# A two-layer decode kernel whose planner gets a new model of transfers, instruction fetches and matmul activity

## The chip, the core and the metric

The kernel runs on one core of a Trainium2 chip. The metric is device time in microseconds (us), lower is better. Every time below is of a whole execution on the device, or comes from one execution taken by the hardware profiler.

## What is computed

Two kinds of layer alternate, A, B, A, B, each added to its input, for 8 sequences of one token (width 448). Both A layers use the same weights and the same caches; so do both B layers.

```python
def _A_ref(x, k_cache, v_cache, wq, wo):      # B=8, 16 query heads, 8 cached heads, 4096 keys, 256 wide
    q = (x @ wq).reshape(B, Sq, Hq, Dh).transpose(0, 2, 1, 3)
    k = jnp.repeat(k_cache, 2, axis=1); v = jnp.repeat(v_cache, 2, axis=1)
    p = _softmax(jnp.einsum("bhqd,bhkd->bhqk", q, k) * Dh ** -0.5)
    o = jnp.einsum("bhqk,bhkd->bhqd", p, v)
    return o.transpose(0, 2, 1, 3).reshape(B, Sq, Hq * Dh) @ wo
def _B_ref(x, w1, w2, w3, w4):
    # the token-mixing part shifts along a sequence of length 1 and so adds nothing
    x1 = x + hs
    return x1 + _gelu(_layernorm(x1) @ w3) @ w4
x = x + _A_ref(_layernorm(x), ...)
x = x + _B_ref(_layernorm(x), ...)
x = x + _A_ref(_layernorm(x), ...)
x = x + _B_ref(_layernorm(x), ...)
```

The caches are large: 8 rows of 8 heads, with 2 MiB of keys and 2 MiB of values for each head, in bfloat16. One row's keys and values are 32 MiB, and both A layers need them.

## The kernel before

**Data.** On chip there is room for 30 quarter slots (`QUARTERS`) of 512 KiB in the tile `kv`; a head's keys or values are four such quarters. A load (`issue_kv`, line 625) fetches one to four quarters of a head that lie side by side, in one transfer of 128 rows. Of each row's eight heads, heads 3 to 7 are "kept": their keys stay on chip from layer 1 to layer 2 (`KEEP_K` 5, but for two quarters that are held otherwise), and so do six quarters of values (`KEEP_V`). Heads 0 to 2 are "free": everything of theirs is loaded for each layer anew.

**Work of one head.** `front` takes keys: TensorE transposes each quarter in two pieces (line 1250) into the tiles `psT`, VectorE or ScalarE copies them back (lines 1233 and 1234), scores follow (line 1045, "scr", 8 matmuls to a group), then maximum, exponentials and sums. `back` takes values: four groups of 8 matmuls (line 1132, "pv"), one for each quarter, then the parts are added (1146, 1148, 1156) and a part of the output projection is made (1181, "wor"). A score group of layer 2, or of a key that isn't kept, frees its quarter slot, and so does each value group of a quarter that isn't kept. The next load into that slot waits for it.

**Between the layers of one row.** After the eighth head of layer 1 the last part of the output projection (`wo_mm`, "wo", lines 985 and 988) closes the row's attention; `mid` then makes sums (731), the MLP's first product (`h_mms`, 56 matmuls at line 839), its second (985, 988), and the queries of layer 2 (823). Only then can layer 2's scores of this row begin. While this goes on, the values of the next row's free heads in layer 1 are loaded and multiplied (`run([("b", 0, b + 1, h) for h in free_heads])`), and then layer 2 of this row starts with its kept heads.

**The planner.** The order of everything is not written out by hand. `Plan.op` records each operation with an estimated time and what it reads and writes; `Plan.schedule` then simulates the engines and puts the operations of each engine into an order. The order is fixed at build time; `synchronise` adds the semaphore waits. A load's size is decided there too: `next_kv` asks for as many quarters as are left of the head and as its `most` allows; it takes them if so many free slots lie side by side before the time `late`, when the transfers issued so far are about to run out, and else takes fewer:

```python
late = max(free["sp"], dma_end - self.LEAD)
...
t = max(late, times[0])
m = min(m, max(k for k, a in runs(t)))
```

The transfers are one queue in this model, with one time `dma_end`. SP (SyncE) issues all loads, in the planned order, so a load that waits holds up those behind it. Fetches of instructions (`fetched`) delay TensorE alone.

**The clock of TensorE.** The planner counts the matmul columns of each window of 3.413 us; above `COLS` it takes the short durations, else the long ones. Where TensorE would stand idle and the count is under `TARGET` it puts in "fillers" (line 1457, "warm"): matmuls whose result nobody reads.

`MOST` is the largest number of quarters in one load of a free head's values in layer 1, for every row but the first.

Of the kernel before, what the change touches and what calls it, by code (L numbers as in the profile page):

```python
# [31 lines left out]
BOOST = None  # L32
HOTK = 7
L2 = (3, 4, 2, 1, 0)
MOST = 4
MOST2 = 4
BACKS = (0, 3, 6)
MIX = "KKKKKFFF"
# [1 line left out]
PV0 = 0  # L40
PV1 = DH
QW, HW, YW = 24, 24, 12
SC = 448
YC = 0
SB, SR = 64, 128
# [30 lines left out]
class Plan:  # L76
# [5 lines left out]
    HOT = 3500  # L82


    ISSUE, LEAD = 4.0, 5.0
    BLOCK, FETCH = 128, 6.0
    LAT = {"pe": 0.25, "dve": 0.06, "act": 0.06, "pool": 0.05, "sp": 0.4}

    def __init__(self):
        self.ops = []  # L90
# [41 lines left out]
    def fetched(self, t, d, n, pairs, next_block):  # L132

        per = d / n
        while n:
            room = self.BLOCK - pairs % self.BLOCK
            if room == self.BLOCK:
                t = max(t, next_block)
                next_block = t + self.FETCH
            k = min(n, room)  # L140
            pairs += k
            n -= k
            t += k * per
        return t, pairs, next_block

    def schedule(self):
        engs = ["pe", "dve", "act", "pool", "sp"]
        free = {e: 0.0 for e in engs}
# [16 lines left out]
        for o in self.ops:  # L165
            if not left[o]:
                release(o, 0.0)
        dma_end = 0.0
        win, cols, warm = 0, 0, False
        recent, hot = [], False  # L170
        bank_ev = {}
# [5 lines left out]
        n = 0  # L177
# [14 lines left out]
        def next_kv(i):  # L192

            u = sp_next[i].unit
            m = 1
            while m < u.most and i + m < len(sp_next) and sp_next[i + m].unit is not None and \
                    sp_next[i + m].unit.tile is u.tile and sp_next[i + m].unit.u == u.u + m and \
                    sp_next[i + m].unit.keep == u.keep:  # L200
                m += 1
            late = max(free["sp"], dma_end - self.LEAD)
            times = sorted(set(x for x in self.free_at if x < 1e9))
            if not times:
                return None
            for t in [max(free["sp"], times[0])] + [x for x in times if free["sp"] < x <= late]:
                fit = [(k, a) for k, a in runs(t) if k >= m]
                if fit:
                    break
            else:  # L210
                t = max(late, times[0])
                m = min(m, max(k for k, a in runs(t)))
                fit = [(k, a) for k, a in runs(t) if k >= m]

            before = sp_next[i - 1].unit if i else None
            if before is not None and before.tile is u.tile:
                for k, a in fit:
                    if a <= before.slot + 1 <= a + k - m:
                        return t, m, before.slot + 1
            k = min(k for k, a in fit)  # L220
            fit = [a for k2, a in fit if k2 == k]
            q = min(fit) if u.keep else max(fit) + k - m
            return t, m, q

        while n < len(self.ops):
            best = None
            for e in engs:
                if e == "sp":
# [5 lines left out]
                    if sp_i < len(sp_next) and sp_next[sp_i] in ready:  # L234
                        t = max(free[e], ready[sp_next[sp_i]])
# [7 lines left out]
                if avail[e]:  # L243
                    t = free[e]
                elif pend[e]:
                    t = max(free[e], pend[e][0][0])
# [4 lines left out]
            t, e = best  # L251
            if e == "sp":
                o = sp_next[sp_i]
# [74 lines left out]
            order[e].append(o)  # L328
            n += 1
            if e == "sp":  # L330
                free[e] = t + 0.45
                start = max(t + self.ISSUE, dma_end)
                dma_end = start + o.dur
                end = dma_end
            else:
                d = o.dur
                if e == "pe":

                    w = int(t / self.WIN)
                    while win < w:  # L340
                        warm = cols >= self.COLS
                        cols = 0
                        win += 1
                    cols += d[2]
                    recent.append((t, d[2]))
                    end, pairs, next_block = self.fetched(t, d[0] if warm else d[1], d[3],
                                                          pairs, next_block)
                    d = end - t
                elif isinstance(d, dict):
                    d = d[e]  # L350
                end = free[e] = t + d
# [109 lines left out]
def bass_interleave_layers__gqa_block_cached__mixer_s_mlp__decode_kernel(  # L461
# [20 lines left out]
    plan = Plan()  # L482
# [117 lines left out]
        return bass.AP(tensor=ap.tensor, offset=ap.offset, ap=[list(x) for x in ap.ap[:-1]] + [[0, P]])  # L600


    FASTER = 1.05

    def dma(name, dst, src, nbytes, sem, val, wr, at, row=8192):

        us = nbytes / 16 / 26.88e3 + nbytes / row / 16 * 0.008
        plan.op("sp", lambda eng: eng.dma_start(dst, src), us / FASTER, name, wr=wr, prio=at,
                dma=(sem, val))

    def dma_once(name, parts, keys, at, also=()):
# [7 lines left out]
    def issue_kv(o, n, q):  # L619

        (cache, b, h), u = o.unit.tile, o.unit.u
        src = cache[b, h].rearrange("(m s) d -> m (s d)", m=P)[:, u * 2048:(u + n) * 2048]
        dst = kv[:, q * 2048:(q + n) * 2048]
        slot_n[q] += 1
        o.emit = lambda eng: eng.dma_start(dst, src)  # L625
        o.dma = (slot_sem[q], 16 * slot_n[q])
        o.dur = ((n << 15) / 26.88e3 + 8 * 0.008) / FASTER

    plan.issue_kv = issue_kv

# [63 lines left out]
    def pe(fn, n, rd=(), wr=(), banks=(), name="chain", prio=None, width=20):  # L694

        if prio is None:
            prio = urge[0] + len(plan.ops)
        d = 0.06 + 0.026 * n
        return plan.op("pe", fn, (d, max(d, 0.06 + n * width / 1200), width * n, n), name, rd=rd, wr=wr, banks=banks, prio=prio)

    def mark(o):

# [298 lines left out]
    def front(layer, b, h, prio=None):  # L1001
# [29 lines left out]
        for u in range(4):  # L1031
            if u in fresh:
                for pc in range(2):
                    bank = transpose_piece(ks[u], pc, u in hold)
                    if u in hold:
                        held.setdefault(u, []).append(bank)

            typ, half = u % 2, u // 2

            def sc(t, typ=typ, q=ks[u]):  # L1040
                last = None
                for c in range(2):
                    w = qb[:, h, c, 2 - 2 * typ:6 - 2 * typ]
                    for g in range(4):
                        last = t.matmul(ps[32 * g:32 * g + 4, SR:SR + DH], w,  # L1045
                                        slot_ap(q, g * 512, 512)[:, c:512:2],
                                        start=(typ == 0 and c == 0), stop=(typ == 1 and c == 1),
                                        skip_group_check=True, tile_position=(0, 32 * g))
                return last
            o = plan.op("pe", sc, (0.25, 0.46, 512, 8), "scr",  # L1050
                    rd=qk + ["q0", ("s", ks[u], 0), ("s", ks[u], 1)],
                    wr=[("sr", half)] + [("sc", par, x) for x in range(u, 4)], banks=[bk],
                    prio=prio and prio + len(plan.ops))
            if layer and h == first2[b] and u == 3:
                o.hot = False
            if u in back_in:
                for pc, bank in enumerate(banks_of[back_in[u]]):
                    evacuate(ks[u], pc, bank).tbank = bank
                    held_banks.remove(bank)
            elif u not in keep_k:  # L1060
                o.frees = ks[u]
            hi = len(plan.ops) - 10 ** 5
            if typ:
                def out_rows(e, half=half):
                    if e is nc.vector:
                        return e.tensor_copy(sR[half][:, :], ps[:, SR:SR + DH])  # L1066
                    return e.copy(sR[half][:, :], ps[:, SR:SR + DH])  # L1067
                plan.op("ev", out_rows, {"dve": 0.42, "act": 0.4}, "evh", rd=[("sr", half)], wr=[("sR", half)],
                        banks=[bk], prio=hi)

                def turn_s(t, half=half):
                    last = None
# [35 lines left out]
    def back(layer, b, h):  # L1108
# [15 lines left out]
        for u in range(4):  # L1124

            def pv(t, u=u, q=vs[u]):
                last = None
                for s in range(8):
# [4 lines left out]
                                    slot_ap(q, s * 256, 256), start=(i < 4), stop=(i >= 28),  # L1133
                                    skip_group_check=True, tile_position=(0, g4))
                return last
            o = plan.op("pe", pv, (0.25, 0.46, 512, 8), "pv",
                    rd=[("pT", nr, 0), ("pT", nr, 1), ("s", vs[u], 0), ("s", vs[u], 1),
                        "pz"],
                    wr=[("pv", par, x) for x in range(u, 4)], banks=[bk])
# [35 lines left out]
        if k < HKV:  # L1175
            def wo_row(t):
                last = None
                for i in range(4):
# [4 lines left out]
                                    stop=(k == HKV - 1 and i >= 2),  # L1183
                                    skip_group_check=True, tile_position=(0, r))
                return last
            o = plan.op("pe", wo_row, (0.41, 0.78, 448, 4), "wor", rd=[("oT", no), "wo0"], wr=[kr],
                        banks=["R"], prio=hi)
            if k == HOTK and layer == 0:
                o.hot = True
# [327 lines left out]
```

## Time and profile before

| | |
|---|---|
| three executions | 1109.34, 1109.49, 1111.36 us (median 1109.49) |
| the profiled execution | 1109.86 us; span of its instructions 1108.1 us |
| TensorE (PE) | busy 970.0 us (88%), granted clock 0.94 of full speed |
| VectorE (DVE), ScalarE (ACT), GpSimd (POOL) | 618.0, 337.3 and 100.1 us |
| read from memory | 438.38 MB, 396 GB/s over the span |
| transfers of instructions | 127 packets, 2.08 MB, 0.8% of the 16 engines' span |
| chain that ended last | PE 51%, DMA 40%, DVE 6% |
| loads of 2048, 1536, 1024 and 512 KiB | 135, 7, 82 and 91 |

The chain that ended last is followed back from the last instruction, at each step to what released it. Busy shares are averages over stages: what bounds a stage is read in windows of it. PE's busy time is modelled from pipelined matmuls, so a busy PE need not be one at its peak.

### The profile page before, as it was taken

Reading aid. Unit: us, or ns where it says so; the run is one execution under the profiler, and the core shown is the slowest. Engines: PE = TensorE matmul, PEld = TensorE weight load, DVE = VectorE, ACT = ScalarE, POOL = GpSimd, SP = SyncE. Lnnn points to the kernel's source line nnn. Section 1 sums busy time; section 2 is a strip of 40 time slices with the busy share of each in tenths; the row PEclk is TensorE's granted clock in tenths of the full one; section 3 lists DMA queues with packets and bytes.
Section 4 is the critical chain, followed back from the end, with each engine's and each line's share of the span. In section 5 each row is a group of like instructions: output and inputs, shape, how many; then the busy total and the mean of one; then the engine's idle time right before and its main releaser. Section 6 shows DMA issues by size and latency. Waiting matters only on the chain.

```text
span 1108.1 us, 36237 instructions
## 1 busy us (share of the span) xinstructions
PE 970.0 (88%) x16253; PEld 673.8 (61%) x16253; DVE 618.0 (56%) x1942; ACT 337.3 (30%) x972; POOL 100.1 (9%) x287
## 2 busy tenths in 40 slices
PE   4899888998989988988989887989888998899886
PEld 3667556665567656666566654667555775476663
DVE  4356455555555655655556555566555564566664
ACT  1134123341334403343134421334132440243130
POOL 0000010000100101010010001010010010101010
PEclk9999989998899989999799999999898897999999
DMA  9999999998999999999999989999999999999993
GB/s 340 408 426 421 395 397 423 424 422 340 418 425 425 423 374 423 426 422 414 355 421 428 422 352 403 422 425 421 364 420 424 426 370 342 419 416 414 364 405 152
DMA packets 49911, 440.72 MB, mean 398 GB/s; under 512 B 5326, under 2 KB 8540, under 8 KB 20700
## 3 DMA queue, kind: packets, MB, share of 16 engines
q1 hardware_dynamic: 49748, 438.41, 96.5%
q8 instruction: 127, 2.08, 0.8%
q14 instruction: 28, 0.23, 0.1%
q10 hardware_dynamic: 8, 0.00, 0.0%
HBM read 438.38 MB, written 0.01 MB: 396 GB/s over the span
## 4 chain that ended last, share of the span: by engine, by line
PE 51%; DMA 40%; DVE 6%; SPq 1%; issue 1%; ACT 0%; POOL 0%; DVEq 0%
DMA kv<-in_A_k_cache_dram 24%; PE psT L1250 23%; DMA kv<-in_A_v_cache_dram 16%; PE psM L1045 9%; PE psP L1132 7%; PE psP L1457 3%; PE psR L1181 2%; DVE oS L1146 1%; PE psM L823 1%; DVE oS L1148 1%; PE psM L985 1%; PE psP L1156 1%; PE psM L1076 1%; PE psM L988 1%; SPq L625 1%
## 5 line engine op out<-in xcount | busy, mean ns | idle before, releaser
L1250 PE MATMUL psT<-ident_f,kv 128*128 128x128 f32 x2816 | 387.2, 285 | 20.1 <-DMA kv<-in_A_k_cache_dram 19.7
L1233 DVE COPY kv<-psT 128x512 f32<-128x512 f32 x394 | 267.9, 690 | 175.4 <-PE psT L1250 149.8
L1250 PEld LDWEIGHTS psT<-ident_f,kv 128*128 128x128 f32 x2816 | 313.1, 144 | 82.3 <-issue 52.2
L1234 ACT COPY kv<-psT 128x512 f32<-128x512 f32 x342 | 197.1, 587 | 305.0 <-PE psT L1250 281.3
L1132 PE MATMUL psP<-kv,pT 128*2 128x256 bf16 x4096 | 175.3, 291 | 22.0 <-DMA kv<-in_A_v_cache_dram 19.4
L1132 PEld LDWEIGHTS psP<-kv,pT 128*2 128x2 bf16 x4096 | 89.6, 86 | 63.8 <-DMA kv<-in_A_v_cache_dram 27.1
L1066 DVE CAST sR<-psM 128x256 bf16<-128x256 f32 x149 | 63.2, 424 | 94.5 <-PE psM L1045 93.0
L1088 POOL PARTITION_ALL_REDUCE gm<-pm x128 | 45.5, 356 | 750.6 <-DVE pm L1086 728.1
L1098 ACT ACTIVATE pT<-sS,nb,fac 128x32 bf16<-128x32 f32 x128 | 52.6, 417 | 180.2 <-DVE nb L1092 180.2
L1045 PE MATMUL psM<-kv,q2T 128*4 128x256 bf16 x2048 | 103.1, 291 | 4.3 <-DVE q2T L1306 2.3
L1045 PE MATMUL psM<-kv,q1b 128*4 128x256 bf16 x2048 | 96.3, 276 | 0.2
L1457 PE MATMUL psP<-ident_f 128*128 128x248 bf16 x473 | 81.4, 289 | 0.0
L1076 PEld LDWEIGHTS psM<-ident_f,sR 128*128 128x128 bf16 x512 | 38.6, 98 | 60.4 <-DVE sR L1066 34.9
L1067 ACT CAST sR<-psM 128x256 bf16<-128x256 f32 x107 | 39.8, 372 | 113.9 <-PE psM L1045 113.9
L1146 DVE CAST oS<-psP 128x256 bf16<-128x256 f32 x128 | 53.9, 421 | 34.4 <-PE psP L1132 33.7
L1181 PE MATMUL psR<-wo_sb,oT 128*1 128x448 bf16 x448 | 67.5, 386 | 3.3 <-DVE oT L1162 3.0
L1076 PE MATMUL psM<-ident_f,sR 128*128 128x16 bf16 x512 | 52.1, 174 | 20.5 <-DVE sR L1066 11.8
L1102 POOL PARTITION_ALL_REDUCE Db<-rs x128 | 51.2, 400 | 188.1 <-ACT pT L1098 188.1
L1156 PE MATMUL psP<-sel,oS 128*128 128x2 bf16 x512 | 32.0, 166 | 32.7 <-DVE oS L1148 31.4
L1045 PEld LDWEIGHTS psM<-kv,q2T 128*4 128x4 bf16 x2048 | 43.1, 85 | 28.7 <-DVE q2T L1306 7.6
L1098 ACT ACTIVATE pT<-sS,nb 128x32 bf16<-128x32 f32 x128 | 40.9, 327 | 52.9 <-DVE nb L1092 52.9
L1148 DVE TENSOR_TENSOR oS<-psP,oS 128x256 bf16<-128x256 f32 x128 | 53.9, 421 | 2.5
(166 smaller groups left out, 737.7 us busy)
## 6 DMA issues: line engine op xcount, KB each, us to landing
kv<-in_A_k_cache_dram SPq DMA_DIRECT2D x69, 2048.0 KB, 23.7
kv<-in_A_v_cache_dram SPq DMA_DIRECT2D x66, 2048.0 KB, 16.4
kv<-in_A_v_cache_dram SPq DMA_DIRECT2D x60, 1024.0 KB, 10.1
kv<-in_A_v_cache_dram SPq DMA_DIRECT2D x77, 512.0 KB, 7.8
kv<-in_A_k_cache_dram SPq DMA_DIRECT2D x22, 1024.0 KB, 15.6
kv<-in_A_k_cache_dram SPq DMA_DIRECT2D x6, 1536.0 KB, 14.0
kv<-in_A_k_cache_dram SPq DMA_DIRECT2D x14, 512.0 KB, 7.3
wo_sb<-in_A_wo_dram SPq DMA_DIRECT2D x1, 3584.0 KB, 45.7
```

Source lines behind the costliest of these rows:

```text
L1045: last = t.matmul(ps[32 * g:32 * g + 4, SR:SR + DH], w, slot_ap(q, g * 512, 512)[:, c:512:2], start=(typ == 0 and c == 0), stop=(typ == 1 ...
L1066: return e.tensor_copy(sR[half][:, :], ps[:, SR:SR + DH])
L1076: last = t.matmul(ps[:, a:a + 16], sR[half][:, j * P:(j + 1) * P], pick, start=True, stop=True)
L1098: return a.activation(pT[nr][:, :, :].rearrange("p i j -> p j i")[:, jj, :], sview[:, jj, :], ACT.Exp, bias=nb[nm][:, jj:jj + 1], scale=sc ...
L1132: last = t.matmul(ps[g4:g4 + 2, PV0:PV0 + DH], pT[nr][:, at, :], slot_ap(q, s * 256, 256), start=(i < 4), stop=(i >= 28), skip_group_check ...
L1146: plan.op("dve", lambda v: v.tensor_copy(oS[:, 0, :], po), 0.36, "o", rd=[("pv", par, x) for x in range(4)], wr=["oS0"], banks=[bk], prio=hi)
L1148: plan.op("dve", lambda v: v.tensor_tensor(oS[:, 1, :], po, oS[:, 0, :], ALU.subtract), 0.36, "o", rd=["oS0"] + [("pv", par, x) for x in r ...
L1181: last = t.matmul(psR[r:r + 1, 0:D], oT[no][:, i % 2, i // 2:i // 2 + 1], wo_sb[:, a:a + D], start=(k == 1 and i < 2), stop=(k == HKV - 1 ...
L1233: return e.tensor_copy(dst, psT[bank][:, :])
L1234: return e.copy(dst, psT[bank][:, :])
L1250: last = t.transpose(psT[bank][:, s * P:(s + 1) * P], src, ident_f[:, :])
L1457: return t.matmul(dst, ident_b, bcast(ident_b[:, 0:n // 4], 4, 1), start=True, stop=True)
```

## The change

The planner's model changes, and with it the order of every engine and the sizes of the loads; no operation's arithmetic does.

- Transfers are 16 engines (`ring`), each with its own free time. A load starts on an engine 1.0 us after its issue or when the engine is free, costs 0.75 us more if the engine had run out of work (`WAKE`), and is usable 0.46 us after the last engine ends (`LAND`). Before, it started 4.0 us after the issue on the one queue. Its duration is set anew, without the divisor `FASTER`. `late` goes by the mean of the 16 times less `LEAD` 4.0.
- Each block of instructions fetched occupies one of eight of these engines in turn (`CARRY`) for 1.55 us.
- `MOST` goes from 4 to 2: the free heads' values of layer 1 are loaded in halves at most.
- In the count of columns a matmul of a chain counts 16 (`CW`) and not its width, a score or value group 568 and not 512, a "wor" group 756 and not 448.
- SP's latency is 0.05 and not 0.4, and its time for an issue 0.4 and not 0.45.

```diff
-MOST = 4
+MOST = 2
+CW = 16
...
-    ISSUE, LEAD = 4.0, 5.0
+    ISSUE, LAND, LEAD = 1.0, 0.46, 4.0
+    RING, CARRY, WAKE = 16, (0, 2, 4, 6, 8, 10, 12, 14), 0.75
+    FETCH_DMA = 1.55
     BLOCK, FETCH = 128, 6.0
-    LAT = {"pe": 0.25, "dve": 0.06, "act": 0.06, "pool": 0.05, "sp": 0.4}
+    LAT = {"pe": 0.25, "dve": 0.06, "act": 0.06, "pool": 0.05, "sp": 0.05}
...
                 next_block = t + self.FETCH
+                c = self.CARRY[self.fetches % len(self.CARRY)]
+                self.fetches += 1
+                self.ring[c] = max(self.ring[c], t + self.ISSUE) + self.FETCH_DMA
...
-        dma_end = 0.0
+        self.ring, self.fetches = [0.0] * self.RING, 0
...
-            late = max(free["sp"], dma_end - self.LEAD)
+            late = max(free["sp"], sum(self.ring) / self.RING - self.LEAD)
...
             if e == "sp":
-                free[e] = t + 0.45
-                start = max(t + self.ISSUE, dma_end)
-                dma_end = start + o.dur
-                end = dma_end
+                free[e] = t + 0.4
+                for i in range(self.RING):
+                    wake = self.WAKE if t + self.ISSUE > self.ring[i] + 0.02 else 0.0
+                    self.ring[i] = max(t + self.ISSUE, self.ring[i]) + wake + o.dur
+                end = max(self.ring) + self.LAND
...
-        o.dur = ((n << 15) / 26.88e3 + 8 * 0.008) / FASTER
+        o.dur = (n << 15) / 27.2e3 + 8 * 0.009
...
-        return plan.op("pe", fn, (d, max(d, 0.06 + n * width / 1200), width * n, n), name, ...)
+        return plan.op("pe", fn, (d, max(d, 0.06 + n * width / 1200), CW * n, n), name, ...)
...
-            o = plan.op("pe", sc, (0.25, 0.46, 512, 8), "scr",
+            o = plan.op("pe", sc, (0.25, 0.46, 568, 8), "scr",
...
-            o = plan.op("pe", pv, (0.25, 0.46, 512, 8), "pv",
+            o = plan.op("pe", pv, (0.25, 0.46, 568, 8), "pv",
...
-            o = plan.op("pe", wo_row, (0.41, 0.78, 448, 4), "wor", ...)
+            o = plan.op("pe", wo_row, (0.41, 0.78, 756, 4), "wor", ...)
```

In the built programs the loads go from 315 to 337: 135 to 130 of 2048 KiB, 7 to 3 of 1536, 82 to 83 of 1024, 91 to 121 of 512. The fillers go from 559 to 651. Line numbers of the changed kernel are five higher from the loads on (L625 is L630, L839 is L844, L1045 is L1050, L1132 is L1137, L1250 is L1255, L1457 is L1462).

More of the change, by code (lines that the diff above doesn't have):

```diff
@@ L600, in wide @@
         return bass.AP(tensor=ap.tensor, offset=ap.offset, ap=[list(x) for x in ap.ap[:-1]] + [[0, P]])
-    FASTER = 1.05
     def dma(name, dst, src, nbytes, sem, val, wr, at, row=8192):
         us = nbytes / 16 / 26.88e3 + nbytes / row / 16 * 0.008
-        plan.op("sp", lambda eng: eng.dma_start(dst, src), us / FASTER, name, wr=wr, prio=at,
+        plan.op("sp", lambda eng: eng.dma_start(dst, src), us, name, wr=wr, prio=at,
                 dma=(sem, val))
@@ L698, in pe @@
         d = 0.06 + 0.026 * n
-        return plan.op("pe", fn, (d, max(d, 0.06 + n * width / 1200), width * n, n), name, rd=rd, wr=wr, banks=banks, prio=prio)
+        return plan.op("pe", fn, (d, max(d, 0.06 + n * width / 1200), CW * n, n), name, rd=rd, wr=wr, banks=banks, prio=prio)
     def mark(o):
@@ L1185, in wo_row @@
                 return last
-            o = plan.op("pe", wo_row, (0.41, 0.78, 448, 4), "wor", rd=[("oT", no), "wo0"], wr=[kr],
+            o = plan.op("pe", wo_row, (0.41, 0.78, 756, 4), "wor", rd=[("oT", no), "wo0"], wr=[kr],
                         banks=["R"], prio=hi)
```

## The prediction

> **What bounds the kernel now.** I read the page's 40 slices first, then what the transfer queue (SP) waited for, then windows by stage, then the chain that ended last at the worst place.
>
> From the page: granted TensorE clock, busy share of the 16 DMA engines, GB/s, each over 40 slices of 27.7 us.
>
> ```profile
> PEclk9999989998899989999799999999898897999999
> DMA  9999999998999999999999989999999999999993
> GB/s 340 408 426 421 395 397 423 424 422 340 418 425 425 423 374 423 426 422 414 355 421 428 422 352 403 422 425 421 364 420 424 426 370 342 419 416 414 364 405 152
> ```
>
> Cache loads bound this kernel: 438 MB at 424 GB/s are 1034 us of a 1108.1 us span. Between the dips the rate stands still at 421 to 428 and nothing on the other engines matters. Time is lost at the start, at the end, and in one dip per batch row, about every 130 us. A dip is where a row leaves layer 1 for layer 2; dip n is that of the nth row.
>
> Windows of 40 us over dips 2 to 8 (a stretch between dips comes first). Columns: window, length, busy us of PE, PEld, DVE, ACT, POOL (with counts), granted clock, DMA busy share, GB/s.
>
> ```profile
> 190.00:240.00 50.00, 46.04 (x650) 33.23 (x642) 28.39 (x74) 20.52 (x55) 4.53 (x12) 1.00 1.00 424
> 250.00:290.00 40.00, 34.44 (x627) 20.11 (x625) 20.97 (x82) 6.99 (x24) 2.48 (x7) 0.79 0.90 360
> 380.00:420.00 40.00, 34.37 (x689) 21.11 (x687) 22.39 (x87) 6.45 (x23) 3.20 (x9) 0.91 0.99 390
> 510.00:550.00 40.00, 35.47 (x620) 21.38 (x619) 20.38 (x83) 6.51 (x21) 2.83 (x8) 0.74 0.93 369
> 640.00:680.00 40.00, 31.77 (x650) 20.30 (x640) 22.13 (x85) 6.90 (x22) 2.82 (x8) 0.91 0.91 361
> 775.00:815.00 40.00, 33.99 (x668) 21.05 (x671) 21.82 (x84) 7.46 (x26) 2.88 (x8) 0.91 0.96 379
> 905.00:945.00 40.00, 35.35 (x648) 22.63 (x647) 21.68 (x85) 8.39 (x28) 2.62 (x7) 0.83 0.95 348
> 1025.00:1065.00 40.00, 36.81 (x756) 26.97 (x755) 24.89 (x94) 10.76 (x28) 2.27 (x6) 0.96 0.98 368
> ```
>
> Loss of a dip against 424 GB/s is 40 x (1 - GB/s / 424): 6.0 us in dip 2, 3.2 in dip 3, then 5.2, 5.9, 4.2, 7.2 and 5.3 in dips 4 to 8. Dip 3 loses least, and that is the key.
>
> The transfer queue's own waits (who, for whom, us in total, times, longest):
>
> ```profile
> SPq L625 <- PE psM L1045: 478.9, 87, 25.3
> SPq L625 <- PE psP L1132: 384.4, 98, 24.4
> ```
>
> Transfers wait for a free quarter slot, which a score (L1045) or value (L1132) matmul group frees on PE. In a dip the kept keys and values hold 24 of 30 slots, so only six circulate.
>
> Four-us windows through the hole of dip 2 and the same place in dip 3 (same columns), then three links of the chain in dip 2:
>
> ```profile
> 262.00:266.00 4.00, 2.99 (x74) 2.08 (x70) 2.19 (x11) 0.00 (x0) 0.00 (x0) 0.97 0.63 262
> 266.00:270.00 4.00, 4.00 (x103) 2.82 (x100) 2.92 (x15) 0.21 (x1) 0.00 (x0) 0.61 0.45 106
> 270.00:274.00 4.00, 3.92 (x101) 3.11 (x101) 1.67 (x11) 0.00 (x0) 0.00 (x0) 0.82 1.00 385
> 394.00:398.00 4.00, 3.52 (x99) 2.87 (x100) 2.05 (x12) 0.00 (x0) 0.00 (x0) 1.00 0.95 356
> 398.00:402.00 4.00, 2.86 (x94) 2.15 (x90) 2.60 (x14) 0.21 (x1) 0.00 (x0) 1.00 0.93 336
> 402.00:406.00 4.00, 4.00 (x81) 2.73 (x84) 1.29 (x8) 0.00 (x0) 0.00 (x0) 0.53 0.99 393
> ```
>
> ```profile
> 265.07 1.65 PE psM L839 x56
> 266.72 1.83 PE psP L1132 x32
> 268.57 7.95 DMA kv<-in_A_v_cache_dram
> ```
>
> Dip 2 loses 4.9 us in these 12 us (1.5 + 3.0 + 0.4), dip 3 1.8. The built order says why. In dip 2 all six slots are filled by one load of four quarters (first free head) and one of two. PE then runs output projection (`wo`), sums and the MLP's 56 matmuls (L839) before any value group, the queue runs dry, and the next transfer leaves only after 266.72 and lands 7.95 us later. In dip 3 the first head came in halves; PE runs two of its value groups before `wo`, so two quarters are on their way under the MLP. Dips 2, 4 and 5 have the form 4+2 and dip 6 the form 4+1+1, all with nothing released before `wo`; dips 3, 7 and 8 have the other form.
>
> **The change part by part.**
>
> *Halves of free heads' values (`MOST` 2) with the new model.* In the order of the changed kernel dips 2, 3 and 4 have the form 2+1+1+1+1, with two value groups of the first free head ahead of `wo` and two quarters released by them; dip 6 has 2+2+1+1, also with two ahead; in dip 5 one group stands ahead and others lie between `wo`, sums and MLP. Two quarters are 1.05 MB, 2.5 us at 424 GB/s. A hole can't be closed below dip 3's level, so the gain in a dip is the smaller of 2.5 and (its loss - 3.2): 2.5 in dip 2 (6.0 - 3.2 = 2.8), 2.0 in dip 4, 2.5 in dip 5 (2.7), 1.0 in dip 6. Sum 8.0 us.
>
> What is late next: the 16 value matmuls now ahead of `wo` push the MLP, the second queries and the scores behind them. Sixteen such matmuls took 0.6 us (0.83 us for 24 at 260.60), in four dips 2.4 us. I charge all of it, since nothing covers PE there; if the queue stays fed it is free, so 0 to 2.4.
>
> *Smaller transfers.* Cache loads go from 315 to 337, quarters from 91 to 121. Each issue holds SP 0.33 us (median of L625), 7 us in all beside 863 us of SP waiting in the two lines above: nothing, unless SP was the late one. The waits that come with them are one PE group for each quarter; behind such a wait on SP stand the next loads in order, and PE's next value groups wait for those. The cost in the engines is read where quarters alone fill the queue:
>
> ```profile
> 804.00:808.00 4.00, 2.67 (x50) 1.24 (x51) 1.36 (x5) 0.37 (x1) 0.35 (x1) 1.00 1.05 419
> ```
>
> Thirty more quarters are 15.7 MB; at 419 in place of 424 GB/s that is 0.4 us. Where the queue is dry, as through dips 7 and 8, quarters pay more; that is the first rival.
>
> The Trainium skill speaks against this part: "DMA: Bandwidth & Descriptors", section Bandwidth, advises at least 1 MiB for a transfer to reach 75% of peak. The row shows 512 KB loads at 419 of 424 GB/s while the queue is full, so the row decides; by the rule's 75% the 15.7 MB would take 12 us longer, as an estimate.
>
> *Transfers and fetches modelled on 16 engines.* No instruction for itself; it moves issues. Counted along the PE order without fillers, the loads released but not yet used fall to 3 quarters at the bottom of dips 2, 4, 5 and 6 before, and to 5 after; dip 3 has 5 in both. Between the dips the changed order keeps somewhat less ahead (20 in place of 24 quarters in dips 2 and 3), with never under 8: 4.2 MB, 10 us of transfers. That costs nothing while transfers end last; I take 0. A stall there would show as a new dip; the window of dip 7, which begins with one (the 303 GB/s of 910 to 915), bounds it at 4 us (7.2 - 3.2).
>
> *Matmul activity taken anew.* Fillers (L1457) grow from 559 to 651, because chain matmuls count as 16 columns each. A filler on the chain took 0.13 us (0.67 us for five at 289.47), so 92 cost 12 us if none were covered. But they are put where the plan expects PE idle, and PE is idle 12% of the span. On the other side the clock stood at 0.79 in dip 2 and 0.74 in dip 4 where dips 3, 5 and 6 had 0.91; PE is busy 34 us of those 40, and what L1132 and L1045 wait for there is mostly a transfer. I take 0, with -3 (dips 2 and 4 at dip 3's speed: their value matmuls are busy 10.89 and 11.73 us, dip 3's 9.95, together 2.7) to +5 (33 us, 3% of the span, run through psP fillers in the chain; 16% more of that).
>
> *Sum.* The profiled execution took 1109.86 us (span 1108.1 and 1.8 around it). 1109.86 - 8.0 + 2.4 + 0.4 = 1104.7. The median of the runs shown is 0.4 lower, so 1104.3.
>
> **The rivals.**
>
> *Quarters starve the queue (slower).* Dip 7 already has the form 2+1+1+1+1 and loses most, 7.2 us: each 512 KB load waits for one PE group, and at 0.83 of the clock the groups come late. If dips 2, 4, 5 and 6 go that way they lose 28.8 in place of 21.3: +7.5, +0.4 for the quarters, 1117.4. It decides from an average dip over 5.3 us (21.3 / 4). Against it: dip 7's window also holds a stall before the hole that has nothing to do with this form, and dip 3 has the same order up to the MLP and 3.2.
>
> *The hole only moves (no change).* The MLP chain sets the length of a dip, whatever is loaded under it. Dip 8, with quarters and no hole, loses 5.3; four such dips are 21.2 against 21.3, so 1109.8 with the quarters. For it: dip 8's share of busy DMA is 0.98 at 368 GB/s. Against it: dip 8 ends the kernel and loads keys there too.
>
> *All of it, and a warmer PE (faster).* 8.0 with nothing given back and 3 from the clock: 1098.5.
>
> That the planner does nothing is excluded: every engine's order differs. Dip 1 and the end are ordered anew as well, but `MOST` doesn't reach the first row and the last loads are quarters in both; I take 0 for them, a us either way.
>
> **How the numbers follow.** The forecast has 0.45, the full gain 0.15, no change 0.16, the starved queue 0.24. About 0.2% or 2.2 us is what a measurement of this kernel can tell from no change. Faster 0.60, same 0.16, slower 0.24. The forecast's own range is 1100 to 1107. For 8 in 10 it reaches down to the full gain, 1098, and up to 1118, past the starved queue's 1117.4.
>
> **What would show it.** Right: dips 2, 4, 5 and 6 at 380 GB/s or more over their 40 us (loss under 4.2), no 4-us window near 106 GB/s, fillers around 650 with a clock of 0.94 or above. Wrong: a window of 100 GB/s or so still under L839, dips at 350 GB/s with busy DMA (quarters), a new dip between rows (lead too short), or a longer time from the last landing to the end, 14 us now.

## The result, and the profile after

The changed kernel took 1117.6 us (median of four runs, 1114.84 to 1118.62) where the kernel before took 1109.4 on the same chip: a ratio of 1.0072, 95% interval 1.0043 to 1.0100. It is slower by some 8 us; I had forecast 1104.3, faster by 5. The profiled run took 1116.98 us, its span is 1115.1 (before 1109.86 and 1108.1).

The page's slices of the kernel after: granted TensorE clock, busy share of the DMA engines, GB/s, 40 slices of 27.9 us.

```profile
PEclk9999899998999998999899998999989998999898
DMA  9999999999999999999999999999999999999893
GB/s 336 411 424 420 393 403 426 424 421 372 414 424 417 404 349 424 426 415 406 350 425 424 422 376 380 422 426 421 368 418 424 424 382 333 424 425 409 299 403 143
```

Lines of the kernel after stand 5 below those of before (L1137 is the old L1132, L630 the old L625). The clock is no lower (0.953 over the span, 0.940 before). The dips are still there, one for each row, and the last one has become the deepest slice between the start and the end, 299 in place of 364 GB/s.

The windows that answer to those shown of before, 40 us over dips 2 to 8, moved by up to 5 us so that each lies over its dip, and a window of 5 us between dips 2 and 3 (same columns: busy us of PE, PEld, DVE, ACT, POOL, granted clock, DMA share, GB/s):

```profile
250.00:290.00 40.00, 32.92 (x669) 19.02 (x667) 20.54 (x84) 5.62 (x19) 2.58 (x8) 0.91 0.99 381
380.00:420.00 40.00, 33.60 (x670) 20.90 (x670) 22.60 (x88) 7.57 (x26) 3.19 (x9) 0.96 0.96 371
513.00:553.00 40.00, 33.89 (x691) 21.64 (x691) 22.13 (x88) 7.80 (x26) 3.23 (x9) 0.91 0.96 362
645.00:685.00 40.00, 34.30 (x658) 20.86 (x650) 22.24 (x87) 7.08 (x23) 2.83 (x8) 0.87 0.97 365
779.00:819.00 40.00, 34.52 (x719) 21.77 (x721) 22.98 (x92) 7.30 (x25) 3.23 (x9) 0.96 0.98 380
908.00:948.00 40.00, 34.35 (x688) 23.05 (x685) 23.68 (x88) 8.67 (x29) 3.02 (x8) 0.91 0.94 362
1027.00:1067.00 40.00, 32.34 (x641) 22.88 (x643) 21.09 (x82) 8.37 (x21) 1.51 (x4) 0.91 0.91 319
360.00:365.00 5.00, 4.42 (x79) 3.54 (x81) 3.48 (x9) 2.57 (x8) 0.75 (x2) 1.00 0.83 305
```

By the prediction's own formula, 40 x (1 - GB/s / 424), dips 2 to 8 now lose 4.1, 5.0, 5.8, 5.6, 4.2, 5.8 and 9.9 us, together 40.4 where before lost 37.0. Dip 2 gained 1.9 and dip 7 1.4; dips 4, 5 and 6 stood still within 0.6; dip 3 lost 1.8 and dip 8 lost 4.6. The last row is new, a dry spot between dips that costs 1.4 us. That is 4.8 of the 7.0 us by which the span grew; 0.8 more lie between the 438th MB and the end (19.0 in place of 18.2), the rest is spread thinly.

The holes of before in dips 2, 4, 5 and 6 are gone: in dips 2 to 6 no 4 us now move less than 227 GB/s. A new one stands in dip 7, just before the MLP's first matmul at 931.16; in that dip the kernel before has no 4 us under 250 GB/s:

```profile
928.00:932.00 4.00, 3.07 (x80) 2.42 (x81) 2.09 (x11) 0.00 (x0) 0.00 (x0) 0.87 0.54 155
```

From the last landing to the end it takes 15.7 us in place of 14.0, and most of the difference is fillers in the chain of waits (first the kernel after, then before; one more filler in each took 0.54 and 0.33 us):

```profile
1101.98 2.15 PE psT L1462 x5
```

```profile
1096.56 0.92 PE psT L1457 x4
```

Dip 8 shows one long stall. Three links of the chain of waits there, then the matching line of PE's timeline (start, us, what; in brackets the idle time before it and who ended it):

```profile
1041.51 0.44 PE psM L1050 x9
1041.95 8.62 DMA kv<-in_A_v_cache_dram
1050.57 0.04 issue
```

```profile
1050.61 0.60 PE L1137 MATMUL psP<-kv,pT 128*2 128x256 bf16 x8 [4.83 <-DMA kv<-in_A_v_cache_dram]
```

A score group at 1041.95 freed the slot for a quarter of values (head 2 of the seventh row, "row 6" in the code, which counts from 0); that quarter took 8.62 us from there to PE, but PE reached the value group at 1045.8 and stood still for 4.83 us, with transposes of the next keys behind it in its order. The kernel before runs that value group 39 groups after the slot is freed, the kernel after runs it 16 groups after.

The chain that ended last, by engine (kernel after; before it was PE 51%, DMA 40%, DVE 6%):

```profile
PE 62%; DMA 25%; DVE 9%; issue 2%; SPq 1%; ACT 1%; POOL 0%; DVEq 0%
```

So in this execution the end is set less by loads and more by PE and the small steps on DVE between PE's groups.

### The profile page after: what moved, and what is told of

It reads as the page before. It is cut to its first block, busy times and chain, and to the rows that moved or that the text cites. A ratio compares the mean times of both kernels' runs of the same rounds, so it can differ in the third digit from the quotient of the medians.

```text
span 1115.1 us, 36455 instructions
## 1 busy us (share of the span) xinstructions
PE 971.6 (87%) x16345; PEld 677.1 (61%) x16345; DVE 624.6 (56%) x1954; ACT 332.5 (30%) x960; POOL 100.0 (9%) x287
## 4 chain that ended last, share of the span: by engine, by line
PE 62%; DMA 25%; DVE 9%; issue 2%; SPq 1%; ACT 1%; POOL 0%; DVEq 0%
PE psT L1255 28%; DMA kv<-in_A_k_cache_dram 16%; PE psM L1050 11%; DMA kv<-in_A_v_cache_dram 9%; PE psP L1137 8%; PE psP L1462 4%; PE psR L1186 3%; DVE oS L1151 2%; DVE oS L1153 2%; PE psM L828 2%; PE psT L1462 1%; PE psP L1161 1%; PE psM L990 1%; DVE sR L1071 1%; PE psM L1081 1%
## 5 line engine op out<-in xcount | busy, mean ns | idle before, releaser
L1255 PE MATMUL psT<-ident_f,kv 128*128 128x128 f32 x2816 | 382.5, 282 | 13.9 <-DMA kv<-in_A_k_cache_dram 13.8
L1238 DVE COPY kv<-psT 128x512 f32<-128x512 f32 x399 | 271.4, 690 | 163.5 <-PE psT L1255 131.7
L1255 PEld LDWEIGHTS psT<-ident_f,kv 128*128 128x128 f32 x2816 | 310.1, 143 | 73.7 <-issue 54.4
L1137 PE MATMUL psP<-kv,pT 128*2 128x256 bf16 x4096 | 168.3, 284 | 12.7 <-DMA kv<-in_A_v_cache_dram 10.6
L1071 DVE CAST sR<-psM 128x256 bf16<-128x256 f32 x156 | 66.2, 424 | 99.5 <-PE psM L1050 98.2
L1137 PEld LDWEIGHTS psP<-kv,pT 128*2 128x2 bf16 x4096 | 88.3, 84 | 48.0 <-DMA kv<-in_A_v_cache_dram 15.8
L1050 PE MATMUL psM<-kv,q2T 128*4 128x256 bf16 x2048 | 105.5, 291 | 6.5 <-DVE q2T L1311 2.6
L1050 PE MATMUL psM<-kv,q1b 128*4 128x256 bf16 x2048 | 97.0, 276 | 3.3 <-ACT kv L1239 1.6
L1462 PE MATMUL psP<-ident_f 128*128 128x248 bf16 x548 | 89.2, 282 | 0.0
L1072 ACT CAST sR<-psM 128x256 bf16<-128x256 f32 x100 | 37.2, 372 | 113.4 <-PE psM L1050 111.6
L1186 PE MATMUL psR<-wo_sb,oT 128*1 128x448 bf16 x448 | 63.7, 367 | 7.5 <-DVE oT L1167 6.2
L1050 PEld LDWEIGHTS psM<-kv,q2T 128*4 128x4 bf16 x2048 | 44.2, 85 | 34.9 <-issue 10.4
L1462 PEld LDWEIGHTS psP<-ident_f 128*128 128x128 bf16 x548 | 45.4, 98 | 26.9 <-issue 21.3
L1161 PEld LDWEIGHTS psP<-sel,oS 128*128 128x128 bf16 x512 | 22.8, 98 | 61.1 <-DVE oS L1153 57.8
```

Of the source, the lines that this page charges most:

```text
L1050: last = t.matmul(ps[32 * g:32 * g + 4, SR:SR + DH], w, slot_ap(q, g * 512, 512)[:, c:512:2], start=(typ == 0 and c == 0), stop=(typ == 1 ...
L1137: last = t.matmul(ps[g4:g4 + 2, PV0:PV0 + DH], pT[nr][:, at, :], slot_ap(q, s * 256, 256), start=(i < 4), stop=(i >= 28), skip_group_check ...
L1161: last = t.matmul(ps[:, PV1 + 2 * c:PV1 + 2 * c + 2], oS[:, w, c:DH:2], sel[:, :], start=(w == 0), stop=(w == 1))
L1186: last = t.matmul(psR[r:r + 1, 0:D], oT[no][:, i % 2, i // 2:i // 2 + 1], wo_sb[:, a:a + D], start=(k == 1 and i < 2), stop=(k == HKV - 1 ...
L1238: return e.tensor_copy(dst, psT[bank][:, :])
L1255: last = t.transpose(psT[bank][:, s * P:(s + 1) * P], src, ident_f[:, :])
```

## The experiments

Each was timed in five rounds beside the kernel before on the same chip; ratios are to that kernel, with 95% intervals. "Quarter" is a load of 512 KB. Where the planner's figures change, it orders every engine anew, so I also moved a figure by a trifle to see how far orders scatter by themselves.

**1. Repairs in place.** The first theory was that the new model lands loads too soon in the plan ("data late"), so the two spots named above make the loss. In `after_pv_late` the changed kernel's order is kept, and only this is edited once it stands:

```
early = [pe[2875], pe[2879]]            # value groups of head 2, row 6
# ... moved some ten groups back, behind transposes of the next keys
self.exchange(sp[332], sp[334])         # next keys' first two quarters take slots
self.exchange(sp[333], sp[335])         # that are free already
```

> The changed kernel's own order, kept as it is except in dip 8: the two value groups of head 2, row 6, for whose data PE stood 4.83 us at 1050.61 are run behind the transposes of the next keys, and the four quarters of the keys after them exchange slots, so that the first two no longer wait for these groups. Theory 'data late' (a plan that thinks loads land sooner than they do puts PE's groups ahead of their data, and everything behind them waits): the stall in dip 8 goes, dip 8 gives back 3 to 5 us, 1112.5 to 1114.5 where the changed kernel has 1117.6. Rival 'quarters' (dip 8 is slow since its loads are of 512 KB): PE waits elsewhere in dip 8 as long, 1116.5 to 1118.5. Rival 'a warmer or colder clock': no change either.

`after_two_fixes` adds one edit: the 2 MB key load that waits at 350 us becomes four quarters, each waiting for its own slot.

```
self.apart(sp[108])
```

> As the run before it, and one load of four quarters at 362 us is issued as four loads of one quarter, each waiting for its own slot alone (three of the four slots had been free for long; the queue ran dry while the load waited for the fourth). Theory 'data late': the window from 360 to 365 us goes from 305 GB/s to above 410 and 1.2 to 1.6 us more come back: 1111.0 to 1113.3. Rival 'lead' (PE is late there whatever the load waits for): the dry spot moves by some us and comes back later, 0 to 0.5 us. Rival 'quarters': four small loads in place of a large one cost, 0 to +1 us.

Measured: 1.0050 (1.0026 to 1.0074) and 1.0057 (1.0031 to 1.0083). Locally both did what they should. The 4.83 us wait is in neither trace, and dip 8 got 2.5 us back: 28 MB from the 406th on took 10.9 us longer than at 425.5 GB/s (the rate that I take for a full queue; its windows show 423 to 426) in the kernel after, 8.3 and 8.4 with the edit. SP's timeline at the second spot, kernel after and then with the split (start, us, what), and the window of the latter:

```profile
350.32 12.10 SPq L630 DMA_DIRECT2D kv<-in_A_k_cache_dram  x2
```

```profile
348.71 0.80 SPq L686 DMA_DIRECT2D kv<-in_A_k_cache_dram  x2
349.55 11.25 SPq L406 DMA_DIRECT2D kv<-in_A_k_cache_dram  x3
```

```profile
360.00:365.00 5.00, 4.01 (x80) 2.49 (x79) 3.62 (x10) 1.33 (x6) 1.02 (x3) 1.00 0.99 402
```

The first line holds two key loads, and the second of them left 12 us after the first: it waited for its fourth slot, though three had been free before, and the queue ran dry. Split, the window has 402 GB/s in place of 305. But the kernel got no faster. Dip 3 right behind it lost 7.9 us (measured as above, 154th to 178th MB), where it had lost 5.9 in the kernel after and 6.3 in `after_pv_late`; that the time came back there is a reading, for a dip of one order varies as much (last section). The two spots are real, but by the ratios the repairs bring back 2.4 and 1.7 us of the 8, and the intervals overlap with the changed kernel's, so that it may be nothing.

**2. One part at a time.** `before_most2` is the kernel before with `MOST = 2`, `after_most4` the changed kernel with `MOST = 4`.

> The kernel before with the halves alone (MOST 2), old transfer model and old activity. My forecast's step: 1109.4 - 8.0 + 2.4 + 0.4 = 1104.2. Theory 'data late': the halves bring 0 to 3 us by themselves: 1106.5 to 1109.5. Rival 'quarters starve the queue': 1113 to 1117.

> Only the halves are undone (MOST 4), the new transfer model and the new matmul activity stay; the planner orders everything anew. My forecast's step (halves worth -8.0, +2.4 and +0.4): the time rises by 3 to 6 us to 1121 to 1124, with windows near 100 GB/s in dips 2, 4, 5, 6 again. Theory 'data late': halves are worth little (-2 in dip 2 alone), and the early value group is still in dip 8: 1116 to 1120. Rival 'quarters starve the queue': 1110 to 1112.

Measured: 1104.03 us, 0.9925 (0.9903 to 0.9948) for the halves alone, and 1.0030 (1.0005 to 1.0055) for all but the halves. The halves alone are faster, as forecast, and by more: the sum of the prediction has 5.2 us. That 1104.03 is the forecast's number is chance, since the kernel before took 1112.63 on that chip and not 1109.4.

`after_most4` went against the forecast's step: without the halves the changed kernel should have lost 3 to 6 us, and it came out no slower, 1.0030 beside 1.0072 (the intervals overlap). Against the kernel before it is not slower than orders scatter (1.0027 for `before_noise` below). So in these orders the halves gain on the old model and not on the new one; whether the new model costs anything without the halves, the scatter hides.

I repeated the first, on another chip:

> The kernel before with the halves alone, unchanged from the run that gave 0.9925, to see whether that holds: 0.990 to 0.996 if the order is the cause; nearer to 1.000 if it was the chip or the hour.

1104.29 us (before on that chip 1111.13), 0.9943 (0.9918 to 0.9969): it holds. Its dips, 40 us each, windows laid as above (profile of `before_most2`):

```profile
250.00:290.00 40.00, 34.22 (x711) 20.69 (x711) 22.30 (x90) 7.05 (x26) 3.24 (x9) 0.91 0.98 389
379.00:419.00 40.00, 33.92 (x686) 20.68 (x685) 22.01 (x86) 7.80 (x26) 3.18 (x9) 0.91 0.97 380
509.00:549.00 40.00, 34.17 (x707) 20.77 (x706) 22.07 (x88) 8.18 (x27) 3.24 (x9) 0.96 1.00 400
637.00:677.00 40.00, 35.66 (x717) 21.82 (x715) 24.21 (x93) 7.67 (x27) 3.64 (x10) 0.91 0.97 384
770.00:810.00 40.00, 33.75 (x674) 20.43 (x676) 21.00 (x84) 7.40 (x25) 2.89 (x8) 0.91 0.98 373
899.00:939.00 40.00, 35.43 (x639) 22.77 (x637) 23.13 (x86) 7.88 (x24) 2.27 (x6) 0.88 0.97 376
1019.00:1059.00 40.00, 36.56 (x690) 25.68 (x690) 23.25 (x87) 9.01 (x23) 1.87 (x5) 0.87 0.89 338
```

Dips 2, 4 and 5 lose 3.3, 2.3 and 3.8 us in place of 6.0, 5.2 and 5.9. Over all seven the loss is 31.0 in place of 37.0, in the second run's profile too. Dip 8 loses 8.1 here and 6.4 there (5.3 before, 9.9 in the changed kernel), so a part of its loss comes with the halves on the old model too, in a kernel that is faster than before.

Then the other two parts: `before_m2_act` is the halves with the new activity figures on the old transfer model, `after_oldact` the halves with the new transfer model and the old activity.

```
before_m2_act:  MOST = 2;  16 * n columns for the chain, 568 / 568 / 756 for scr, pv, wor
after_oldact:   width * n columns for the chain, 512 / 512 / 448
```

> The kernel before with the halves and the new matmul activity, on the old transfer model. The halves alone were 0.75% faster than before, the whole change is 0.5 to 0.7% slower, so the other two parts take back some 13 us between them. Theory 'transfer model': it takes nearly all of it, so this kernel stays near the halves alone, 0.990 to 0.995 of before. Rival 'activity' (fillers and clock): 1.000 to 1.007 of before. Rival 'luck of a plan' (any new plan scatters by half a per cent): anything from 0.992 to 1.007, without a pattern over this call's four kernels.

> The changed kernel with the old matmul activity: halves and the new transfer model. Theory 'transfer model': as slow as the changed kernel, 1.003 to 1.008 of before. Rival 'activity': 0.990 to 0.996.

0.9971 (0.9948 to 0.9993) and 1.0043 (1.0019 to 1.0068). `before_m2_act` and the changed kernel (1.0072) differ in the transfer model alone: 1.0%, 11 us, in this pair of orders.

**3. How far orders scatter.** A rate moved by 0.2%, in three kernels:

```
before_noise, before_m2_noise:  FASTER = 1.052   (was 1.05; the second with MOST = 2)
after_noise:                    (n << 15) / 27.25e3   (was 27.2e3)
```

> The kernel before with its rate moved by 0.2% (1.052), nothing else. It measures how far another order out of the same rules lies from the kernel before: within 0.3% (0.997 to 1.003) if the order before is an ordinary one, 1.003 to 1.008 if it is a lucky one.

> The halves alone once more, with one constant of the plan moved by 0.2% (transfers 1.052 in place of 1.05 times faster than the formula), so that the planner finds another order out of the same rules. Theory 'halves work': 0.990 to 0.995 of before again. Rival 'luck of a plan': 0.996 to 1.005.

> The changed kernel with one constant of the plan moved by 0.2% (27.25 in place of 27.2 for a transfer's rate); the early value group of dip 8 isn't in this order. Theory 'transfer model' (a fault of the rules): still slow, 1.002 to 1.008 of before. Rival 'luck of a plan': below 1.000.

1.0027 (1.0000 to 1.0054), 0.9997 (0.9972 to 1.0023) and 1.0025 (1.0001 to 1.0049). Two orders out of the same rules lie 0.3 to 0.7% apart. The order before was a fairly good one, `before_most2` is a very good one, the changed kernel a poor one. Still the groups don't mix: the old transfer model with halves gave 0.993 (mean of the two runs), 0.997 and 1.000; the new one 1.0072, 1.0043, 1.0025 and, with one figure moved below, 1.0023, 1.0024 and 1.0051. The means of the first three on each side lie 0.8% apart, 9 us; the nearest two of all, 0.9997 and 1.0023, only 0.3%, and their intervals overlap.

**4. Which figure of the transfer model.** Three figures, put back or taken out one at a time, in the changed kernel or in the halves alone, and two of them together:

```
after_issue3:         ISSUE = 3.0   (1.0; a quarter lands 5.5 us after its issue in the plan, not 3.5)
after_nofetch:        FETCH_DMA = 0 (1.55)
after_faster:         every planned transfer / 1.05
before_m2_slow:       MOST = 2, FASTER = 1.0 (1.05)
after_faster_issue3:  ISSUE = 3.0 and every planned transfer / 1.05
```

> The changed kernel with the planner's time from an issue to the first byte at 3.0 us in place of 1.0, so that a quarter lands 5.5 us after its issue into an idle queue, as in the old model (5.6), and not 3.5. All else as changed. The early value group of dip 8 isn't in this order. Theory 'data late' (the new latency is too short): 0.992 to 0.999 of before. Rival 'another part of the transfer model' (fetches in the rings, the lead rule, the slower rate): still 1.002 to 1.007.

> The changed kernel without instruction fetches on the modelled engines (1.55 us each to 0). The planner then places 575 fillers in place of 651. Theory 'fetches make the plan's queue late, so PE is planned idle and filled': 0.993 to 1.000 of before. Rival 'data late': unchanged or worse, 1.002 to 1.008.

> The changed kernel with every transfer planned 1.05 times faster, as the old model had it (4.66 us for 2 MB in place of 4.89); all else of the new model stays. The planner places 495 fillers and 159 quarter loads. Theory 'rate' (a plan whose queue runs faster than the real one keeps the real one fed): 0.990 to 0.998 of before. Rival 'quarters': slower than the changed kernel, 1.008 or more. Rival 'scatter': 1.000 to 1.007.

> The kernel before with the halves, and transfers planned at the formula (1.0 in place of 1.05 times faster): the old latency, the old lead rule, no fetches, 94 quarter loads, 716 fillers. Theory 'rate': the gain of the halves is gone, 1.002 to 1.008 of before. Rival 'quarters' (there are as few as in the fast ones): 0.992 to 0.998. Rival 'the rest of the new model': 0.992 to 0.998 too.

> The changed kernel with both old figures of a load put back, its rate (1.05 times faster) and its latency (issue to first byte 3.0 in place of 1.0 us); rings, fetches and the lead rule stay new. 93 quarter loads and 512 fillers, as the old model with halves has them. Theory 'rate and latency together': 0.992 to 0.999 of before. Rival 'the rings, fetches or the lead rule': 1.002 to 1.007.

Latency alone 1.0023 (1.0000 to 1.0047), no fetches 1.0024 (1.0003 to 1.0045), rate alone 1.0051 (1.0025 to 1.0077): none returns the gain by itself, and each moves the changed kernel by 0.2 to 0.5%, no more than orders scatter. The rate taken out of the old model: 1.0054 (1.0027 to 1.0081), the halves' gain gone; that is 1.1 and 1.3% over the two runs of `before_most2`, but 0.6% over the other order out of the same rules (0.9997). Rate and latency put back together: 0.9994 (0.9967 to 1.0021), 0.8% under the changed kernel, though 0.5 to 0.7% over the halves alone. The chain by engine, in this order `before_most2`, `before_m2_slow`, `after_faster_issue3`:

```profile
DMA 50%; PE 42%; DVE 5%; SPq 1%; issue 1%; ACT 0%; POOL 0%; DVEq 0%
```

```profile
PE 63%; DMA 22%; DVE 11%; issue 2%; ACT 1%; SPq 1%; POOL 0%; DVEq 0%
```

```profile
PE 49%; DMA 42%; DVE 7%; SPq 1%; issue 1%; ACT 0%; POOL 0%; DVEq 0%
```

With transfers planned at the rate of the formula, PE has most of the chain (63%, and 62% in the changed kernel); planned 5% faster than that, loads have 42 to 50% of it. The share does not decide: `after_faster` has 46% DMA and is slow all the same, with 159 quarters and a clock of 0.925, and `after_nofetch`, planned at the formula's rate, has 43%.

**5. The two costs that the prediction priced.** `m2_split` leaves the order and waits of `before_most2` as they are and issues each load of two or three quarters as that many quarters:

```
k = n if n in (2, 3) else 1
for x in range(k):  eng.dma_start(part x of dst, part x of src)   # same semaphore
```

> The kernel before with the halves (0.9925 of before), its order and its waits unchanged, but every load of two or three quarters is issued as two or three loads of one quarter right after one another: 90 quarter loads become some 276. It prices the size alone. Theory 'size': a dip pays for each small load; if the 30 more quarters of the changed kernel are its 8 us, 186 more cost over 20 us, 1.01 of before or more. Theory 'waits, not size': 0.990 to 0.996 as without the split.

1.0006 (0.9982 to 1.0031). The issues of value quarters in `before_most2` and in the split one (count, KB, median us to landing):

```profile
kv<-in_A_v_cache_dram SPq DMA_DIRECT2D x84, 512.0 KB, 7.4
```

```profile
kv<-in_A_v_cache_dram SPq DMA_DIRECT2D x224, 512.0 KB, 9.2
```

With the keys 186 more quarters cost 0.72% over the mean of the two runs of `before_most2`, 8.0 us: 0.04 us each. Size does cost, against what I expected, but the 30 of the change make 1.3 us of its 8. "DMA: Bandwidth & Descriptors" of the Trainium skill, section Bandwidth, asks for at least 1 MiB for 75% of peak; 186 quarters are 97.5 MB, 230 us at 424 GB/s, and by that rule 77 us more, as an estimate. Nearly ten times what the split cost here, where the queue holds several loads at a time.

The fillers, in the changed kernel's own order, every sixth or every second one left out:

```
drop = every 6th (after_fill_56) or every 2nd (after_fill_half) of the "warm" groups
```

> The changed kernel's own order, with every sixth filler left out (542 of 651, about as many as the kernel before has); fillers compute nothing that is used. Theory 'fillers on the path' (the chain of the changed kernel runs 5% through fillers, before 3%): a sixth of 5% is 9 us, the time falls to 0.997 to 1.001 of before. Rival 'loads come late' (fillers stand where PE would wait for its data anyway): unchanged, 1.003 to 1.007 of before. Rival 'clock' (fewer fillers cool PE): slower than that, with a clock under 0.94.

> The same with every second filler left out (325 of 651). 'Fillers on the path': 20 us and more come back unless the clock falls, 0.985 to 0.995 of before. 'Loads come late': 1.003 to 1.007. 'Clock': 1.01 to 1.03, clock 0.90 or lower.

1.0084 (1.0060 to 1.0107) and 1.0162 (1.0134 to 1.0191). The clock of the second, from the spans by core:

```profile
core 0: 1124.9 us, clock 0.892
```

Fillers pay: 326 fewer cost 0.9%, 10 us, and the clock falls from 0.953 to 0.892. With 109 fewer it is 0.929, and the 0.1% that they cost is not clear of noise. They stand on the chain, yet leaving out a part of them gains nothing.

## Why the prediction was wrong, step by step

**What bounds the kernel, and the hole.** Right. In dip 2 of the kernel before the queue issues nothing from 10.0 us before the MLP's first matmul to 2.2 after it; in the kernel after two quarters leave 1.6 and 0.8 us before it, and the 4 us from 266 on (the MLP begins at 264.04, before at 265.07) move 321 GB/s in place of 106:

```profile
266.00:270.00 4.00, 2.81 (x76) 1.72 (x68) 1.93 (x11) 0.21 (x1) 0.00 (x0) 1.00 0.91 321
```

**Halves: -8.0 in dips 2, 4, 5 and 6, and +2.4 and +0.4.** About right as a price of the halves alone, wrong as a price of the change. Alone they gave 2.7, 2.9 and 2.1 us in dips 2, 4 and 5 (I had 2.5, 2.0, 2.5) and lost 0.6 in dip 6 (a gain of 1.0); the profile of the second run has 2.3, 1.1 and 1.4, and -0.5. In all they gained 8.3 and 6.3 us by the ratios, where the sum has 5.2; that is partly a lucky order, for another one out of the same rules came to 0.9997. The 2.4 was not measured by itself. In the changed kernel the same dips gained 1.9, -0.6, 0.3 and 0.0. I read the form of each dip from the changed order and took its price from the order before, as if all around it stayed.

**The quarters, +0.4.** Too small: 30 x 0.04 is 1.3 us. I read it in a stretch with a full queue, and said that a dry queue pays more without pricing it.

**Transfers and fetches on 16 engines: "I take 0".** This is the step that failed. With the halves and the new activity on both sides, the transfer model alone is worth 11 us (0.9971 to 1.0072), 9 between the means of three orders each, and the 4 us that I gave as its bound are less than half of either. Without the halves it is not seen to cost more than orders scatter (`after_most4`). I judged it by the loads in flight, 20 against 24 quarters between dips and 5 against 3 at the bottom, and found nothing to pay. That count says how many quarters are on their way, not whether PE is where the plan has it. A dry spot between dips came as I had named it (305 GB/s at 360 us, 1.4 us), and removing it did not shorten the kernel; for the larger part I found no place of its own. Averaged over dips 2 to 8, the 5 us before the MLP's first matmul lose 0.93 us against 425.5 GB/s in the changed kernel, 0.29 before, 0.56 in both runs of the halves alone; the ten us from 5 after it lose 2.13, 1.49, and 1.35 and 1.69.

PE's waits (who, for whom, us in total, times, longest) point the same way. Kernel after, then `before_most2`:

```profile
PE psP L1161 <- DVE oS L1153: 39.9, 57, 1.3
PE psT L1255 <- DMA kv<-in_A_k_cache_dram: 13.8, 10, 2.9
```

```profile
PE psP L1156 <- DVE oS L1148: 32.0, 54, 1.0
PE psT L1250 <- DMA kv<-in_A_k_cache_dram: 31.3, 30, 3.7
```

The changed order has PE wait less for keys and more for DVE's small steps. Read with the chain's 62%, PE runs later in it and the slots come free later; this is argued, not shown, and `after_faster`, slow as well, waits 32.5 us for keys and 28.7 for DVE. That rate and latency of the plan make the loss together rests on one order, 0.9994, just beyond the scatter of orders: likely, not shown. Why a plan with a queue 5% faster than the formula orders PE better is not settled, nor whether the last 0.5% to the halves alone are the rings, the fetches, the lead rule, the activity or the scatter of orders.

**Activity, 0 (-3 to +5).** The two pairs that differ in it say 0.9934 to 0.9971 and 1.0043 to 1.0072, 3 to 4 us slower, each no more than orders scatter; inside the bounds, not shown. My reason for more fillers was false: I had fillers grow because chain matmuls count as 16 columns. On the old model the new figures took 535 fillers to 484; the rate made them, 716 with `FASTER` 1.0 and 495 with the rate back in the changed kernel.

**The signs I had named.** Fillers at 651 and a clock of 0.953 came, as I wanted for a faster kernel. Windows near 106 GB/s went from dips 2, 4 and 5, but one of 155 came in dip 7; 380 GB/s came in dips 2 and 6 alone. Of the signs for wrong the new dip between rows came, and the longer time from the last landing to the end (15.7 us in place of 14.0). The clock told nothing on the outcome.

**The rivals.** "Quarters starve the queue" gave 1117.4 and came within 0.2 us, by another cause: of its 8 us the quarters' size is 1.3, and with `MOST = 4` the new model has 112 quarters, 21 more than before, at 1.0030. "The hole only moves" is true of the repair at 360 us alone. My chance for the slower side was 0.24, and all of it hung on quarters; an order that suits the chip less, a likely harm of a change to a planner's figures, had no place among the rivals.

The best version here is the kernel before with the halves alone, 0.9925 and 0.9943 of before.

## What to carry to other kernels

Where a planner writes the order, a change to its cost model is a part of the change like any other, and a structural edit priced in the old order is not yet priced in the new one: build each part alone. Orders out of the same rules differed by 0.3 to 0.7%, so judge a planner's figure by several orders, with something irrelevant moved a little, before the figure is called better or worse. A model meant to be nearer to the machine need not make the better order. Here transfers planned 5% faster than the formula gave the faster kernel in all three pairs, by 0.6 to 1.3% on the old model with halves and by 0.2 and 0.3% on the new one, where orders scatter as much.

## What the hardware showed that I had not expected

One program's executions lie further apart than its dips differ: `after_pv_late` ran from 1112.3 to 1123.6 us in twelve, and dip 5, ordered alike in three kernels, lost 7.2, 9.8 and 9.3 us (40 MB from the 250th on, less their time at 425.5 GB/s). A dip read in one profile is uncertain by a us or two, a whole quarter of what I priced.

A page of the Trainium skill, "TensorE: Matmul & The Clock Gate", Part 1, says that the window in which the clock gate counts activity runs free and that a kernel's cold matmuls vary from run to run; no run here shows whether that makes this spread.

A quarter among many others lands later: in `m2_split` quarters of values take 9.2 us from issue to landing at the median, in place of 7.4, and those of keys 12.8; the plan of the changed kernel has 3.5 us for a quarter into an empty queue (1.0 + 0.75 + 1.28 + 0.46), and the one in dip 8 took 8.6 from the release of its slot.
